# A scratch tensor in DRAM re-laid in two parts, and one more channel-major quarter in every third block, in a ConvNeXt-V2 block

## The chip, the cores and the metric

One core of a Trainium2 chip runs the whole program. The metric is device time in microseconds (us). Engines: PE (matmuls), DVE (vector), ACT (ScalarE), POOL (GpSimd), and SP (SyncE), which computes nothing and here issues most DMAs.

## The reference

```python
# x: (1, 512, 512, 96) bf16; dw: (3, 3, 96); w1: (96, 384); w2: (384, 96)
out = depthwise_conv3x3(x, dw)                       # zero padding
h = layernorm(out, axis=-1)
h = gelu(einsum('bhwc,ce->bhwe', h, w1))
gx = sqrt((h * h).sum(axis=(1, 2)) + 1e-6)           # over all pixels, per channel of 384
nx = gx / (gx.mean(axis=-1) + 1e-6)
h = grn_gamma * (h * nx) + grn_beta + h
return x + einsum('bhwe,ec->bhwc', h, w2)
```

The sum over all pixels forces two phases. Phase 1 makes everything up to the GELU and sums the squares. Phase 2 multiplies by `w2`, once the sums are known.

## The kernel before

The image is 128 blocks of four rows (`GR = 4`); a block's 2048 pixels are four quarters of 512. Phase 1 writes the normalised activations `yn` to DRAM. It reads them back transposed, with channels on the partitions, and does the first matmul and the GELU on all four quarters. One quarter's GELU output is kept in DRAM (`g_dram`); phase 2 makes the other three again from `yn`. (The last two blocks keep two quarters in SBUF.)

The squares are summed in two ways. For a *channel-major* quarter, DVE runs batch-norm statistics over its pixels. For a *pixel-major* quarter, PE multiplies the output by its own transpose (a Gram matrix, of which the diagonal counts). Two or three quarters of a block are channel-major:

```python
    def cm_quads(q):
        return 3 if q % 3 and not is_res(q) else 2
    def yn_src(q):
        return yn_dram[q].rearrange("c (r w) -> c r w", r=GR)
    def yn_rows(q):                       # what phase 2 reads: 128 x 4 runs of 768 bytes
        k = kept_quads(q) * 128
        return yn_dram[q:q + 2].rearrange("q c (r w) -> (q c) r w", r=GR)[0:128, :, k:]
    def yn_dst(q, r):
        return yn_dram[q].rearrange("(c i) (r w) -> r c i w", i=NI, r=GR)[r]
    # ...
        def stage_write(b):               # yn has partition 32 * r + c, then i, then w
            yn = yns.pop(b)
            for r in range(GR):
                sp.dma_start(out=yn_dst(b, r), in_=yn[32 * r:32 * r + 32, :, :])
        def stage_read(b):
            t = yn_ring[b % NYT]
            sp.dma_start(out=t[:C], in_=yn_src(b))
```

The work is software-pipelined in slots. SyncE's DMAs in the order of the program (shortened):

```python
            if s + 4 < NBLK:
                load_x(s + 4)                       # one DMA
            for b in get("read"):  stage_read(b)    # one DMA: the block written a slot ago
            for b in get("write"): stage_write(b)   # four DMAs
            for k in get("bcast"): stage_bcast(k)   # every fourth slot: four DMAs, 1/std to all partitions
            for k in get("rows"):  stage_rows(k)    # every fourth slot: two DMAs
            if store: store()                       # one DMA: the kept GELU output
```

## Time and profile before

The median is 1568.49 us. These lines of the profile page give busy time and share of the span for each engine, then, in 40 slices of the span, the clock granted to PE and the busy share of the 16 DMA engines, in tenths.

```profile
span 1563.2 us, 55720 instructions
PE 1450.2 (93%) x23749; PEld 844.8 (54%) x23749; DVE 1129.5 (72%) x2027; ACT 1447.1 (93%) x1306; POOL 1314.2 (84%) x933
...
PEclk9999999999999999999999999999999999999999
DMA  5668787787778677777778667869999999999993
```

The stretch from 300 to 900 us lies in phase 1, that from 1250 to 1450 us in phase 2. Columns: stretch, length, busy time of each engine (instructions), granted clock, DMA share, GB/s.

```profile
300.00:900.00 600.00, 563.83 (x10229) 283.10 (x10213) 517.70 (x878) 562.14 (x560) 532.24 (x397) 1.00 0.77 234
```

```profile
1250.00:1450.00 200.00, 197.63 (x2786) 143.72 (x2785) 104.68 (x196) 197.06 (x146) 188.35 (x116) 1.00 1.03 388
```

PE and ACT are both 94% busy in phase 1. The legend of the page warns that a busy PE isn't a PE at its peak, so look at ACT. Its timeline (start, duration, what it made, count, idle time before) shows one block per `y_bf`:

```profile
407.33 1.45 ACT L32 ACTIVATE y_bf<-Y 128x1536 bf16<-128x1536 f32 x1
408.67 2.93 ACT L32 ACTIVATE gm<-U 128x1024 bf16<-128x1024 f32 x3
412.15 2.92 ACT L32 ACTIVATE gsh<-U 128x1024 bf16<-128x1024 f32 x3 [0.55 <-PE U L32]
414.97 1.45 ACT L32 ACTIVATE y_bf<-Y 128x1536 bf16<-128x1536 f32 x1
...
422.44 1.45 ACT L32 ACTIVATE y_bf<-Y 128x1536 bf16<-128x1536 f32 x1
...
429.88 1.45 ACT L32 ACTIVATE y_bf<-Y 128x1536 bf16<-128x1536 f32 x1
```

The blocks take 7.64, 7.47 and 7.44 us: ACT does seven operations nearly back to back. One slot in three is slower, by 0.17 us. SyncE's own timeline (SPq) of two blocks:

```profile
425.91 0.41 SPq L32 DMA_DIRECT2D g_dram<-gsh  x1
426.36 0.44 SPq L32 DMA_DIRECT2D xin<-in_x_dram  x1
426.98 0.33 SPq L32 DMA_DIRECT2D ynT<-yn_dram  x1
427.35 2.55 SPq L32 DMA_DIRECT2D yn_dram<-yn  x4
429.94 2.29 SPq L32 DMA_DIRECT2D rbc<-r_dram  x4
432.33 0.86 SPq L32 DMA_DIRECT2D g_dram<-gsh  x1
433.29 0.38 SPq L32 DMA_DIRECT2D xin<-in_x_dram  x1
433.77 0.43 SPq L32 DMA_DIRECT2D ynT<-yn_dram  x1
434.25 2.49 SPq L32 DMA_DIRECT2D yn_dram<-yn  x4
```

Each write of yn takes SyncE about 0.6 us to issue. SyncE isn't counted in the busy table at all; only this timeline shows how full it is. These are its waits from 300 to 900 us (total us, times, longest):

```profile
SPq L32 <- DMA yn_dram<-yn: 73.5, 63, 4.7
SPq L32 <- POOL yn L32: 42.2, 22, 4.0
SPq L32 <- DVE rt L32: 19.7, 14, 1.9
```

Its instructions cover 381 of these 600 us, and its waits come to 205: it has slack.

### The profile page before, as it was taken

What the parts mean: (1) busy time and instruction counts of PE and PEld (TensorE: products, weight loads), DVE (VectorE), ACT (ScalarE), POOL (GpSimd) and SP (SyncE); (2) the same over time, 40 slices, a digit from 0 to 9 for tenths busy, and PEclk for the clock granted to TensorE, in tenths of its full rate; (3) what the DMA queues carried; (4) which work ended last, traced back from release to release, by engine and by line L of the source; (5) the groups of instructions that cost most, each with busy time, mean ns of one, the idle gap of its engine ahead of it and who ended that gap; (6) DMA issues with size and microseconds to landing.
All of it is one profiled execution on the core that took longest, in us unless ns stands there. A gap on an engine that the chain in (4) does not pass through costs nothing. (4 is left out here: it accounts for less than half of the span.)

```text
span 1563.2 us, 55720 instructions
## 1 busy us (share of the span) xinstructions
PE 1450.2 (93%) x23749; PEld 844.8 (54%) x23749; DVE 1129.5 (72%) x2027; ACT 1447.1 (93%) x1306; POOL 1314.2 (84%) x933
## 2 busy tenths in 40 slices
PE   7888999999999999999999997789999999999997
PEld 3444444444444444444444444457777777777765
DVE  6748978888898888889888888855555555555544
ACT  3889989999999999999999999989999999999997
POOL 3559888998989898998889897459999999999994
PEclk9999999999999999999999999999999999999999
DMA  5668787787778677777778667869999999999993
GB/s 148 182 182 269 224 262 217 240 254 227 225 234 259 210 249 244 230 235 237 247 210 243 213 197 230 268 238 387 393 379 396 387 397 388 383 381 388 379 372 147
DMA packets 235470, 427.94 MB, mean 274 GB/s; under 512 B 34102, under 2 KB 148374, under 8 KB 235222
## 3 DMA queue, kind: packets, MB, share of 16 engines
q1 hardware_dynamic: 219972, 356.59, 70.2%
q0 software_dynamic: 13888, 67.64, 11.4%
q8 instruction: 186, 3.05, 0.8%
q14 instruction: 62, 0.51, 0.1%
q10 hardware_dynamic: 1362, 0.15, 0.1%
HBM read 272.78 MB, written 150.72 MB: 271 GB/s over the span
## 5 line engine op out<-in xcount | busy, mean ns | idle before, releaser
L32 PE MATMUL U<-ynT,w1p 128*128 128x512 bf16 x2166 | 603.1, 380 | 43.5 <-ACT gm L32 8.7
L32 DVE BATCH_NORM_STATS2 bst<-gsh 128x6 f32<-128x512 bf16 x756 | 468.7, 673 | 128.9 <-ACT gsh L32 128.4
L32 ACT ACTIVATE gr<-U 128x1536 bf16<-128x1536 f32 (+1 forms) x384 | 521.0, 1450 | 17.3 <-PE U L32 14.6
L32 POOL TENSOR_TENSOR yn<-y_bf,rbc 128x1536 bf16<-128x1536 bf16 x128 | 396.9, 3103 | 81.0 <-ACT rbc L32 29.7
L32 DVE TENSOR_TENSOR o_sb<-O,xb 128x384 bf16<-128x384 f32 x512 | 277.5, 557 | 252.2 <-PE O L32 179.7
L278 POOL TENSOR_TENSOR xb<-xr,B2c 128x1536 f32<-128x1536 bf16 x126 | 394.9, 3134 | 43.4 <-DVE B2c L32 35.2
L32 ACT ACTIVATE gsh<-U 128x1024 bf16<-128x1024 f32 x378 | 369.4, 1024 | 55.8 <-ACT gm L32 29.6
L32 ACT ACTIVATE gm<-U 128x1024 bf16<-128x1024 f32 x384 | 368.1, 1035 | 0.6 <-PE U L32 0.5
L32 PE MATMUL Y<-xT,Wq 64*32 64x511 bf16 (+1 forms) x8694 | 320.9, 388 | 9.8 <-DVE B2bc_f L32 3.7
L32 POOL TENSOR_TENSOR ysq<-y_bf 128x1536 bf16<-128x1536 bf16 x114 | 313.2, 2748 | 14.0 <-ACT y_bf L32 13.4
L32 PEld LDWEIGHTS <-w1p 128*128 128x128 bf16 x2166 | 169.4, 97 | 277.9 <-issue 174.2
L32 PEld LDWEIGHTS <-gr 128*128 128x128 bf16 x4584 | 228.7, 98 | 84.4 <-ACT gr L32 12.1
L32 PE MATMUL O<-W2s,gr 128*128 128x96 bf16 x4584 | 251.3, 206 | 12.1 <-ACT gr L32 9.4
L32 PEld LDWEIGHTS <-Wq 64*32 64x32 bf16 x9216 | 102.2, 90 | 187.5 <-issue 146.9
L32 PE MATMUL U<-w1p,ynT 128*128 128x384 bf16 (+2 forms) x1032 | 161.3, 272 | 33.7 <-ACT gm L32 30.6
L32 ACT ACTIVATE y_bf<-Y 128x1536 bf16<-128x1536 f32 x121 | 175.1, 1447 | 16.6 <-PE Y L32 16.4
L32 DVE STREAM_TRANSPOSE xT<-xin 128x576 f32<-128x576 f32 (+1 forms) x256 | 181.2, 747 | 3.2 <-DMA xin<-in_x_dram 3.1
L32 DVE BATCH_NORM_STATS2 bst<-gm 128x6 f32<-128x512 bf16 x252 | 156.5, 676 | 0.9 <-ACT gm L32 0.9
L32 PEld LDWEIGHTS <-ynT 128*128 128x128 bf16 x1032 | 88.7, 96 | 90.8 <-issue 69.4
L32 PE MATMUL SG<-gm 128*128 128x128 bf16 x2064 | 136.3, 219 | 0.5 <-ACT gm L32 0.3
L32 PEld LDWEIGHTS <-gm 128*128 128x128 bf16 x2064 | 121.0, 98 | 11.5 <-issue 0.5
L250 POOL DMA_DIRECT2D xr<-in_x_dram x123 | 67.6, 549 | 27.6 <-POOL xb L278 27.6
(103 smaller groups left out, 700.3 us busy)
## 6 DMA issues: line engine op xcount, KB each, us to landing
ynT<-yn_dram SPq DMA_DIRECT2D x254, 384.0 KB
xin<-in_x_dram SPq DMA_DIRECT2D x126, 432.0 KB
yn_dram<-yn SPq DMA_DIRECT2D x512, 96.0 KB
xr<-in_x_dram POOLq DMA_DIRECT2D x128, 384.0 KB, 6.6
out_dram<-o_sb SPq DMA_DIRECT2D x127, 384.0 KB
g_dram<-gsh SPq DMA_DIRECT2D x126, 384.0 KB
gl<-g_dram SPq DMA_DIRECT2D x84, 384.0 KB
gl<-g_dram POOLq DMA_DIRECT2D x42, 384.0 KB, 6.4
```

Source lines behind the costliest of these rows:

```text
L32: r = f(*a, **k)
L250: pq.dma_start(out=xr[:], in_=x[0, r0:r0 + GR].rearrange("r w c -> (r w) c").rearrange("(p g) c -> p g c", g=PXP))
L278: pq.tensor_tensor(out=xb[:], in0=grp[q]["xr"][:], in1=bias[:, None, :].to_broadcast([128, PXP, C]), op=ALU.add)
```

## The change

The intent is twofold. The three quarters that phase 2 needs are stored together, so that phase 2 reads 3 KB runs instead of 768 B ones. And every block (but the last two) has three channel-major quarters, which takes 42 quarters of Gram work off PE. The diff, cut to its core:

```diff
     def cm_quads(q):
-        return 3 if q % 3 and not is_res(q) else 2
+        return 2 if is_res(q) else 3
@@
     def yn_rows(q):
-        k = kept_quads(q) * 128
-        return yn_dram[q:q + 2].rearrange("q c (r w) -> (q c) r w", r=GR)[0:128, :, k:]
+        n = GR * (NQ - kept_quads(q)) * 128
+        return yn_dram[q:q + 2].rearrange("q c w -> (q c) w")[0:128, :n]
-    def yn_dst(q, r):
-        return yn_dram[q].rearrange("(c i) (r w) -> r c i w", i=NI, r=GR)[r]
+    def yn_dst(q, r):
+        k = kept_quads(q) * 128
+        n = GR * (W - k)
+        dst = yn_dram[q].rearrange("(c i) w -> c i w", i=NI)
+        return [(slice(k, W), dst[:, :, r * (W - k):(r + 1) * (W - k)]),
+                (slice(0, k), dst[:, :, n + r * k:n + (r + 1) * k])]
@@
             for r in range(GR):
-                sp.dma_start(out=yn_dst(b, r), in_=yn[32 * r:32 * r + 32, :, :])
+                for cols, dst in yn_dst(b, r):
+                    sp.dma_start(out=dst, in_=yn[32 * r:32 * r + 32, :, cols])
 (cut: the same re-indexing where the matmuls read the tile)
```

A row's write is now two DMAs, one of 384 columns and one of 128.

More of the change, by code (lines that the diff above doesn't have):

```diff
@@ L101, with quad, pixel_cols @@
     MB = W // PXP
-    def quad(flat_ap, t):
-        return flat_ap.rearrange("p r (t g m) -> p t g r m", t=NQ, m=MB)[:, t]
+    def quad(yt, b, t):
+        k = kept_quads(b)
+        n = GR * (NQ - k) * 128
+        part, t, m = (yt[:, n:], t, k) if t < k else (yt[:, :n], t - k, NQ - k)
+        return part.rearrange("p (r t g m) -> p t g r m", r=GR, t=m, m=MB)[:, t]
+    def pixel_cols(b, r, t):
+        k = kept_quads(b)
+        return (r * (NQ - k) + t - k) * 128
     def quad_out(flat_ap):
         return flat_ap.rearrange("p (g r m) -> p g r m", r=GR, m=MB)
-    def yn_src(q):
-        return yn_dram[q].rearrange("c (r w) -> c r w", r=GR)
     def yn_rows(q):
+        n = GR * (NQ - kept_quads(q)) * 128
+        return yn_dram[q:q + 2].rearrange("q c w -> (q c) w")[0:128, :n]
+    def yn_dst(q, r):
         k = kept_quads(q) * 128
-        return yn_dram[q:q + 2].rearrange("q c (r w) -> (q c) r w", r=GR)[0:128, :, k:]
-    def yn_dst(q, r):
-        return yn_dram[q].rearrange("(c i) (r w) -> r c i w", i=NI, r=GR)[r]
+        n = GR * (W - k)
+        dst = yn_dram[q].rearrange("(c i) w -> c i w", i=NI)
+        return [(slice(k, W), dst[:, :, r * (W - k):(r + 1) * (W - k)]),
+                (slice(0, k), dst[:, :, n + r * k:n + (r + 1) * k])]
     consts = ctx.enter_context(tc.tile_pool(name="consts", bufs=1))
@@ L146 @@
     NYT = 6
-    yn_ring = [prepool.tile([128, GR, W], bf16, name=f"ynT{i}") for i in range(NYT)]
+    yn_ring = [prepool.tile([128, GR * W], bf16, name=f"ynT{i}") for i in range(NYT)]
     ynts = {}
@@ L212 @@
         for t in yn_ring:
-            pool.dma_start(out=t[C:128, :, :], in_=zrow[C:128, None, :].to_broadcast([128 - C, GR, W]))
+            pool.dma_start(out=t[C:128, :].rearrange("p (r w) -> p r w", w=W),
+                           in_=zrow[C:128, None, :].to_broadcast([128 - C, GR, W]))
         dve.tensor_copy(out=ident_b[:], in_=ident_f[:])
@@ L247, in stage_load @@
                 ynt = yn_ring[v]
-                sq.dma_start(out=ynt[:, :, kept_quads(q) * 128:], in_=yn_rows(q))
+                src = yn_rows(q)
+                sq.dma_start(out=ynt[:, :src.shape[1]], in_=src)
             xr = late.xr.tile([128, PXP, C], bf16, name="xr")
@@ L266, in fresh @@
                     pe.matmul(quad_out(U[:, t - nk, :]), lhsT=w1p[:, j * 128:(j + 1) * 128],
-                               rhs=quad(ynt[:], t), start=True, stop=True)
+                               rhs=quad(ynt[:], q, t), start=True, stop=True)
                 n = (NQ - nk) * QW
@@ L591, in stage_write @@
             for r in range(GR):
-                sp.dma_start(out=yn_dst(b, r), in_=yn[32 * r:32 * r + 32, :, :])
+                for cols, dst in yn_dst(b, r):
+                    sp.dma_start(out=dst, in_=yn[32 * r:32 * r + 32, :, cols])
         def stage_read(b):
             t = yn_ring[b % NYT]
-            sp.dma_start(out=t[:C], in_=yn_src(b))
+            sp.dma_start(out=t[:C], in_=yn_dram[b])
             ynts[b] = t
@@ L616, in cm_mm @@
             def cm_mm(dst, j, t):
-                pe.matmul(quad_out(dst), lhsT=w1p[:, j * 128:(j + 1) * 128], rhs=quad(yt[:], t), start=True, stop=True)
+                pe.matmul(quad_out(dst), lhsT=w1p[:, j * 128:(j + 1) * 128], rhs=quad(yt[:], b, t), start=True, stop=True)
             def pair(j):
@@ L637, in rest @@
                         t, r = divmod(k, GR)
-                        col = (cm_quads(b) + t) * 128
-                        pe.matmul(Uf[:, c - c0:c - c0 + sz], lhsT=yt[:, r, col:col + 128], rhs=w1p[:, e0:e0 + sz],
+                        col = pixel_cols(b, r, cm_quads(b) + t)
+                        pe.matmul(Uf[:, c - c0:c - c0 + sz], lhsT=yt[:, col:col + 128], rhs=w1p[:, e0:e0 + sz],
                                   start=True, stop=True)
```

## The prediction

> **What bounds the kernel now.** Phase 1 (to about 1035 us) is a loop over 128 row blocks. ScalarE's timeline from 400 to 450 us shows a block every 7.45 us where three quarters are channel-major, every 7.63 us where two are. The stretch 400 to 600 us has ScalarE 187.2 of 200 us busy, PE 188, POOL 177, DVE 172. ScalarE's work is the floor there, and the change doesn't touch it. In phase 2 ScalarE is 99.9% busy (1100 to 1300 us) with 128x1536 GELUs 1.37 us apart, PE full, POOL 94%, DMA share 1.03, 4.1 us a block.
>
> **What the change removes.** In 42 blocks a pixel-major quarter turns channel-major: 504 Gram matmuls (219 ns each) go. At most the slower block falls to the faster: 42 x 0.17 = 7 us. Phase 2 reads yn in 128 packets of 3072 B (121 ns) instead of 512 of 768 B (37 ns): 0.2 us of 16 engines a block; the share falls to about 0.98. ScalarE stays the floor, so I count 0 to 5 us, after 1300 us, where it is 98% busy.
>
> **What it adds.** (a) 126 batch-norm statistics on DVE, 0.60 us apart: 76 us. A block with three channel-major quarters takes about 7.2 of 7.45 us of DVE: it fits, barely. (b) The write of yn becomes eight DMAs a block instead of four, all issued by SyncE in program order. In its timeline four take 2.5 us (0.64 apart), with the same 96 rows each. SyncE's issue work per block is about 4.6 us (write 2.5, three large DMAs 0.4 to 0.45 each, every fourth block 2.1 for the rstd broadcast and 1.2 for its rows) and becomes about 7.2. And SyncE also stands still: it reads block b-1 back only when its write has landed, 1.8 to 5.8 us after the last issue (waits), with only 0.9 us of issues between. Each DMA also waits for a semaphore last used eight DMAs earlier (instruction order). (c) Half of the write packets are 256 B; the Trainium skill, "DMA: Bandwidth & Descriptors", Specifications, says that below 512 B there is a read-modify-write; no run here shows it yet. The DMA share of phase 1 (0.77) has room.
>
> The Trainium skill, "Perfetto Trace Analysis", What "DMA-bound" means, names this case: the issuing sequencer solid with DMA slices. SyncE isn't now; I expect it to be.
>
> **Critical path.** SyncE per block after: write 5.1, read 0.4, landing wait 1 to 1.5 not overlapped, store and x load 0.9, semaphores 0.2: 7.8 in a plain block, 8.8 with the broadcast, 8.1 on average: 0.6 over today for some 105 blocks (+60), about 1.2 for the last 15, which run at 6 us without the convolution (+18). The gain in phase 1 is hidden; phase 2 gives back 3. Sum: about +70 us.
>
> **Prediction: 1635 us, range 1578 to 1700. Faster by over 2%: 0.03; within 2%: 0.25; slower: 0.72.**
>
> **What would show it.** Phase 1 ends near 1110 us; phase 2 keeps its length within 5 us. SyncE's timeline is solid, writes 0.6 us each, its wait for the yn write the largest. ScalarE and PE fall to about 87% in phase 1; PE waits for the yn read. DVE rises to 90%, no higher.
>
> **What would make it wrong.** The 256 B writes issue faster than 0.6 us or land in under 2 us: within 2%. DVE's work delaying the transposes, or slow 256 B writes: worse than said. ScalarE held by DMA in phase 2: faster there.

## The result and the profile after

The changed kernel takes 1724.35 us (1720.07 to 1725.76, four runs); before took 1568.49. The ratio is 1.0991, 95% interval 1.0969 to 1.1012: slower. (Ratios are the mean time of one kernel's fast runs over that of the other's of the same rounds, so not quite the ratio of the medians.) The direction was right. The time lies above the range of 1578 to 1700, and the loss is 156 us where 70 was forecast.

The page after:

```profile
span 1723.2 us, 55251 instructions
PE 1481.7 (86%) x23119; PEld 835.0 (48%) x23119; DVE 1206.7 (70%) x2157; ACT 1455.4 (84%) x1306; POOL 1313.2 (76%) x933
...
PEclk8999999999999899999999999989999999999999
DMA  5557667777666677767777675576999999999994
```

The same two stretches after:

```profile
300.00:900.00 600.00, 505.31 (x8511) 240.59 (x8495) 487.77 (x827) 490.88 (x485) 461.20 (x350) 0.94 0.70 204
```

```profile
1250.00:1450.00 200.00, 200.00 (x2840) 146.91 (x2839) 108.60 (x200) 199.65 (x148) 188.36 (x115) 1.00 1.02 390
```

In phase 1 every engine in the busy table does less per microsecond, and so do the DMA engines: the limit is none of them. SyncE's timeline after:

```profile
520.49 0.54 SPq L32 DMA_DIRECT2D g_dram<-gsh  x1
521.12 1.64 SPq L32 DMA_DIRECT2D xin<-in_x_dram  x1
523.56 0.32 SPq L32 DMA_DIRECT2D ynT<-yn_dram  x1
523.93 5.04 SPq L32 DMA_DIRECT2D yn_dram<-yn  x8
529.07 1.17 SPq L32 DMA_DIRECT2D r_dram<-rt  x2
530.35 0.41 SPq L32 DMA_DIRECT2D g_dram<-gsh  x1
530.80 0.43 SPq L32 DMA_DIRECT2D xin<-in_x_dram  x1
531.41 0.33 SPq L32 DMA_DIRECT2D ynT<-yn_dram  x1
531.78 5.90 SPq L32 DMA_DIRECT2D yn_dram<-yn  x8
537.73 1.98 SPq L32 DMA_DIRECT2D rbc<-r_dram  x4
```

It is all but solid: its instructions cover 512 of the 600 us from 300 to 900 (381 before), and its waits come to 72 us instead of 205. The waits for `yn` from POOL and for `rt` from DVE are gone from the list. What is left is led by the landing of its own DMAs:

```profile
SPq L32 <- DMA xin<-in_x_dram: 16.9, 19, 2.3
SPq L32 <- DMA yn_dram<-yn: 12.4, 19, 2.3
SPq L32 <- DMA ynT<-yn_dram: 8.4, 28, 0.4
```

The other engines' waits show how SyncE's lateness spreads. GpSimd waits for the 1/std broadcast (`rbc`), which SyncE issues behind eight writes; PE and DVE then wait for GpSimd:

```profile
POOL yn L32 <- DMA rbc<-r_dram: 70.8, 10, 8.2
...
DVE rt L32 <- POOL rstd L32: 63.0, 17, 5.0
PE SG L32 <- POOL ysq L32: 61.5, 30, 3.2
```

The ends of each block's last phase 1 GELU in ACT's timeline give the time by part (us):

| part | before | after | forecast of the difference |
|---|---|---|---|
| to the end of the 5th block (ramp) | 112.7 | 116.6 | none |
| next 108 blocks, each | 7.57 | 8.79 (+132 in all) | +0.6 each, +60 |
| last 15 blocks (no convolution), each | 5.95 | 7.70 (+26 in all) | +1.2 each, +18 |
| phase 2 | 543.4 | 542.0 | 0 to -5 |

### The profile page after: what moved, and what is told of

Same layout as the page of the kernel before. It is cut to its first block, busy times and chain, and to the rows that moved or that the text cites. A ratio compares the mean times of both kernels' runs of the same rounds, so it can differ in the third digit from the quotient of the medians.

```text
span 1723.2 us, 55251 instructions
## 1 busy us (share of the span) xinstructions
PE 1481.7 (86%) x23119; PEld 835.0 (48%) x23119; DVE 1206.7 (70%) x2157; ACT 1455.4 (84%) x1306; POOL 1313.2 (76%) x933
## 5 line engine op out<-in xcount | busy, mean ns | idle before, releaser
L32 PE MATMUL U<-ynT,w1p 128*128 128x512 bf16 x2292 | 657.9, 387 | 72.1 <-ACT gsh L32 29.3
L32 ACT ACTIVATE gm<-U 128x1024 bf16<-128x1024 f32 x384 | 375.8, 1032 | 109.2 <-PE U L32 107.5
L32 PEld LDWEIGHTS <-w1p 128*128 128x128 bf16 x2292 | 181.1, 98 | 337.4 <-issue 229.4
L32 PE MATMUL Y<-xT,Wq 64*32 64x511 bf16 (+1 forms) x8694 | 329.9, 398 | 10.2 <-DVE B2bc_f L32 3.7
L32 DVE BATCH_NORM_STATS2 bst<-gm 128x6 f32<-128x512 bf16 x378 | 234.6, 676 | 1.7 <-ACT gm L32 1.7
L32 PE MATMUL U<-w1p,ynT 128*128 128x384 bf16 (+2 forms) x780 | 144.2, 300 | 29.0 <-ACT gm L32 27.6
L32 PE MATMUL SG<-rowsel,ysq 128*128 128x4 bf16 x1536 | 57.7, 167 | 108.5 <-POOL ysq L32 108.4
L32 PE MATMUL SG<-gm 128*128 128x128 bf16 x1560 | 123.2, 236 | 0.6 <-DVE SG L32 0.3
L32 PEld LDWEIGHTS <-ynT 128*128 128x128 bf16 x780 | 79.9, 106 | 72.6 <-issue 51.7
L32 PEld LDWEIGHTS <-gm 128*128 128x128 bf16 x1560 | 106.8, 107 | 14.3 <-issue 5.2
```

The costliest lines, as they stand in the source:

```text
L32: r = f(*a, **k)
```

## The experiments

Theory A: the doubled number of DMAs that SyncE must issue sets the pace. Rival B: the added statistics on DVE do. Rival C: the small write packets do. Later came theory D about a loop. Times are medians; each ratio is against runs of the kernel before in the same session.

**e1_cm_only** is the kernel before with the new `cm_quads` alone (the first hunk of the diff).

> The kernel before with three channel-major quarters in every block and nothing else changed: four writes of yn a block, old layout. Theory A (the doubled number of DMAs that SyncE must issue sets the pace of phase 1): 1558 to 1572 us, since only the up to 7 us of the faster blocks can be won. Rival B (the 126 added statistics on DVE fill it and hold up the transposes and the GELU buffers): well above 1600 us, most of the way to 1724. Rival C (small 256 B write packets): as A.

Measured: 1556.89 us, ratio 0.9937 (0.9922 to 0.9951). The median lies just under the 1558 of theory A. In the profiled runs phase 1 ends 7.0 us earlier, the very number that 42 times 0.17 us gave, but in part by luck: the middle 108 blocks give 3.2 of it, the last 15 give 2.5 and the ramp 1.3. Its stretch shows DVE at 95%, ACT as before, and the clock full:

```profile
300.00:900.00 600.00, 555.00 (x9906) 262.82 (x9905) 570.38 (x969) 565.26 (x565) 536.83 (x403) 1.00 0.76 236
```

B is refuted: this half of the change is a small gain.

**e2_layout_only** is the changed kernel with the old `cm_quads`.

> The changed kernel with the old rule of two or three channel-major quarters; the layout and its eight writes a block stay. Theory A: 1715 to 1735 us, as the changed kernel. Rival B (DVE): about 1568 us. Rival C (256 B packets): as A, so this run doesn't tell A from C.

Measured: 1721.05 us, ratio 1.0983. The whole loss is in the half of the change that re-lays yn, with its eight writes.

**e3_split512** is the kernel before with nothing changed but the count of writes:

```diff
             for r in range(GR):
-                sp.dma_start(out=yn_dst(b, r), in_=yn[32 * r:32 * r + 32, :, :])
+                for h in range(2):
+                    cols = slice(256 * h, 256 * h + 256)
+                    sp.dma_start(out=yn_dst(b, r)[:, :, cols], in_=yn[32 * r:32 * r + 32, :, cols])
```

> The kernel before with each write of yn cut in two halves of 256 columns: eight DMAs a block, packets of 512 B, none smaller, old layout, old rule, no contiguous reads. Theory A: 1700 to 1735 us. Rival C (packets of 256 B are slow to write and land late): 1568 to 1590 us. Rival B: 1568.

Measured: 1726.38 us, ratio 1.1019. The old layout, no packet below 512 B, and the same loss: C is refuted as the cause of the loss. A write of 96 KB (before) takes SyncE 597 ns (median), one of 48 KB (here) 596, and the mix of 72 and 24 KB (after) 596. The cost goes by the DMA, not by the byte. (By the number of runs in DRAM it doesn't go either: see e5.)

**e4_one_write** has the new `cm_quads`, and yn laid out in DRAM as row, channel, column. SBUF partition 32r + c and the index i then map to one contiguous DRAM row of 3 KB, so one DMA writes the block:

```diff
-    yn_dram = dram.tile([NBLK, C, GR * W], bf16, name="yn_dram")
+    yn_dram = dram.tile([NBLK, GR, C, W], bf16, name="yn_dram")
+    # read: yn_dram[q].rearrange("r c w -> c r w"); phase 2 the same, [:, :, k:], 96 rows
-            for r in range(GR):
-                sp.dma_start(out=yn_dst(b, r), in_=yn[32 * r:32 * r + 32, :, :])
+            sp.dma_start(out=yn_dram[b].rearrange("r (c i) w -> (r c) (i w)", i=NI), in_=yn[:].rearrange("p i w -> p (i w)"))
```

> Three channel-major quarters in every block, and yn laid out in DRAM as row, channel, column: the write is one DMA of 128 contiguous rows of 3 KB, the read back 384 runs of 1 KB. SyncE issues three large DMAs a block instead of six before and ten after, about 2.8 us of issue work. Theory A: not slower than before, 1545 to 1568 us, ScalarE the floor of phase 1; SyncE mostly idle. Rival B (DVE): above 1600 us. If the DMA engines or the landing of the write were the limit, it would be no better than before.

Measured: 1568.31 us (1556.17 to 1576.20), ratio 1.0005: a hair above the bounds of theory A, and not what I hoped. Phase 1 ended at 1006.0 us (before 1019.8), but phase 2 took 559.7 instead of 542 to 543. The next batch has the cause (e8).

**e5_kept_merged** is the changed kernel with the kept part in an array of its own, written by one DMA a block and read by one:

```diff
+    yk_dram = dram.tile([NBLK, GR, C, 256], bf16, name="yk_dram")
-        return [(slice(k, W), dst[:, :, r * (W - k):(r + 1) * (W - k)]),
-                (slice(0, k), dst[:, :, n + r * k:n + (r + 1) * k])]
+        return [(slice(k, W), dst[:, :, r * (W - k):(r + 1) * (W - k)])]
+            sp.dma_start(out=yk_dram[b][:, :, :k].rearrange("r (c i) w -> (r c) i w", i=NI), in_=yn[:, :, :k])
+            # and a second read, yk_dram[b][:, :, :k].rearrange("r c w -> c r w"), in stage_read
```

> The changed kernel, still with 256 B packets for the kept quarter (now also read back in 256 B runs), the contiguous 3 KB reads of phase 2 and three channel-major quarters; but the kept part of the four rows goes into its own array with one DMA. A block has five writes and two reads instead of eight and one: seven DMAs of yn instead of nine (five before). Theory A (SyncE's issue time): SyncE needs 5 x 0.64 + 2 x 0.4 + 0.9 + 0.9, about 5.8 us and 0.5 to 1 of waits, under the 7.4 of ScalarE: 1552 to 1580 us. Theory C (256 B packets): stays above 1680. Contiguous reads in phase 2 worth something: at or under 1555.

Measured: 1567.60 us, ratio 1.0005. More 256 B packets than in the changed kernel, the same contiguous reads, the same DVE work, two DMAs a block fewer: the loss is gone but for about 11 us. (The fair comparison is e1, with as many channel-major quarters and 1556.89 us; whether the two DMAs that e5 still has over e1 or the small packets cost these 11 us, no run tells.) Phase 2 took 542.4 us, so the contiguous reads are worth about nothing. The run also parts the number of DMAs from the number of runs: the one write of the kept part, 384 runs of 256 B, took SyncE 598 ns (median), as long as a write of 96 runs.

**e6_split6** is as e3, with only two of the four rows cut in halves.

> The kernel before with six writes a block (two rows cut in halves of 256 columns, two whole): the dose between four (1568) and eight (1726). Theory A as a threshold: SyncE needs about 6.7 us of issue and dispatch and some waits, just at today's 7.5 us a block: 1565 to 1605 us. If each added DMA cost the same whatever the slack, it would be half way, 1645.

Measured: 1601.62 us, ratio 1.0217 (1.0195 to 1.0238). Two more DMAs cost 33 us and four cost 158 (against the 1568.49 of before). The dose isn't proportional, as expected, but the time lies at the upper end of what I wrote: SyncE begins to cost before the ledger below shows it full.

**e7_read_later** is the changed kernel with the read back a slot later, so that SyncE doesn't stand before a write it has only just issued:

```diff
-                put(s + 2, "read", b)
+                put(s + (2 if ramp or is_res(b) else 3), "read", b)
```

> The changed kernel with the read back of a block moved one slot later in SyncE's order, so that SyncE no longer stands still for the landing of the write it has just issued. If the landing wait is a good part of the loss, as the prediction's sum had it (1 to 1.5 us a block): 1590 to 1660 us. If the issue work alone fills the block (512 of 600 us in DMA instructions plus about 0.04 us between them, 91%): 1690 to 1724 us.

Measured: 1706.47 us, ratio 1.0893. The wait for the landing, in which the prediction saw its extra, is worth 18 us of 156. In the profiled runs the middle blocks fell from 8.79 to 8.56 us, 25 us in all; the ramp, now deeper, lost 10.

**e8_one_write_128** is e4, with phase 2 reading 128 rows again (the last 32 land where the weights are zero):

```diff
-        return yn_src(q)[:, :, k:]                     # 96 rows
+        d = yn_dram[q]
+        return bass.AP(d.tensor, d.offset + k, [[W, 128], [C * W, GR], [1, W - k]])
```

> The one-write version, whose phase 1 ended at 1006 us but whose phase 2 took 560 us instead of 542, with the phase 2 read over 128 rows again (32 rows of them read in vain, as before) instead of 96. If the 96-row read made the transfers slow: phase 2 back at 542, 1545 to 1553 us in all. If the row, channel, column layout in DRAM did: 1562 to 1575 us again.

Measured: 1552.02 us (1550.05 to 1553.46), ratio 0.9904 (0.9888 to 0.9920): 1% faster than the kernel before, 10% faster than the changed one. Phase 2 is back at 542.0 us. The stretch of phase 2 in e4, then in e8:

```profile
1250.00:1450.00 200.00, 191.99 (x2717) 140.27 (x2715) 103.49 (x192) 191.88 (x142) 184.83 (x113) 1.00 1.04 353
```

```profile
1250.00:1450.00 200.00, 197.61 (x2779) 143.44 (x2776) 104.44 (x196) 197.06 (x145) 188.34 (x116) 1.00 1.03 386
```

The DMA engines are full in both and moved 9% less with the 96-row read. In the trace's packet records (1100 to 1500 us) a 3072 B packet took 137 ns on average with it and 124 without, a 768 B packet 42 and 37. Why, no run tells.

**e9_x_by_scalar** is the changed kernel with the load of x issued by ACT from block 8 on (`(sp if b < 8 else act).dma_start(...)`).

> The changed kernel with the load of x (one DMA a block from block 8 on) issued by ScalarE instead of SyncE; bytes, packets, layout and all other DMAs as in the changed kernel. Theory A: SyncE is relieved of 0.45 us of issue and 0.05 of dispatch a block, so about 115 blocks each shorten by 0.4 to 0.55: 1655 to 1685 us, although ScalarE, the floor of the kernel before, gets more to do. If the loss were in the DMA engines, in packet sizes or in landing times: unchanged, 1715 to 1730.

Measured: 1800.02 us, ratio 1.1478: a miss, in the wrong direction. SyncE's waits (300 to 900 us) tell of it:

```profile
SPq L32 <- DMA xin<-in_x_dram: 83.9, 44, 4.8
SPq L32 <- DMA yn_dram<-yn: 26.9, 47, 2.7
```

The framework gives the DMAs issued by SyncE and by ACT eight completion semaphores in turn, and a DMA must wait until the one eight before it has landed. The instruction listing of the changed kernel shows this (shortened; DMAHW0 to 7 are the eight):

```
g_dram<-gsh 128x1536 [waits DMAHW7,Activation]
xin<-in_x_dram 128x1728 [waits DMAHW0,DVE]
ynT<-yn_dram 96x2048 [waits DMAHW2,DMAHW1,PE]
yn_dram<-yn 96x1x384 [waits Pool]
yn_dram<-yn 96x1x128 [waits DMAHW3]
yn_dram<-yn 96x1x384 [waits DMAHW4]
```

With the x loads in ACT's program order, SyncE waits for ACT to reach them. So e9 is no fair test of A.

**e10_one_write_oldcm** is e8 with the old `cm_quads`.

> The one-write layout with the 128-row read of phase 2, and the old rule (two or three channel-major quarters). It completes a square: before 1567, three quarters alone 1557, one write and three quarters 1552. If the two gains add: 1560 to 1564 us. If the one write alone brings nothing, since SyncE had slack: 1566 to 1569.

Measured: 1566.14 us (1560.96 to 1574.77), ratio 1.0000 (0.9975 to 1.0024). One write alone brings nothing, since SyncE had slack. With three channel-major quarters it brings about 5 us over e1. That small interaction stays unexplained.

**e11_fill** is the changed kernel with a matmul repeated in each of the three GELU pairs (`cm_mm(U[:, 0, :], j, 0)` once more).

> The changed kernel with one of the first two matmuls of each GELU group done twice (three more 128x512 matmuls a block, same result), to keep the tensor engine busier: its granted clock fell from 1.00 to 0.94 in phase 1 of the changed kernel. Theory A: the lower clock follows from the idle tensor engine and costs nothing: 1718 to 1732 us, whether or not the clock rises. If the clock were a cause of the loss: a higher clock and a time clearly under 1710.

Measured: 1728.12 us, ratio 1.1042. The granted clock rose from 0.94 to 0.97 in the same stretch, and the time stayed:

```profile
300.00:900.00 600.00, 534.28 (x8704) 252.70 (x8697) 489.21 (x830) 491.39 (x485) 460.25 (x345) 0.97 0.70 205
```

The lower clock after the change came with an idler PE, and it isn't a visible cause of the loss.

**e12_x_by_pool** is as e9, but the x loads are issued by GpSimd, whose DMAs have semaphores of their own.

> The changed kernel with the load of x issued by GpSimd, whose DMAs use semaphores of their own (in the earlier try ScalarE's x loads took their turns among SyncE's eight semaphores, and SyncE stood waiting for them 84 of 600 us). SyncE has 0.5 us a block less to issue. Theory A, issue work plus a nearly constant wait: a block of 8.2 to 8.4 us instead of 8.8, 1660 to 1690 us in all. If SyncE's issue isn't what sets the pace: unchanged, 1715 to 1730.

Measured: 1733.90 us (1725.42 to 1744.66), ratio 1.1072: above both ranges, and again no gain. SyncE's issue work fell by 0.35 us a block, and its waits rose by 0.5. The wait before the read went from 0.22 to 0.68 us a block: the x load's issue had been filling the time in which the write lands. GpSimd also got more to do, so this isn't a clean test of A either.

**e13_more_buffers** is the changed kernel with four buffers for `yn` and `gsh` instead of three.

> The changed kernel with four buffers instead of three for yn in SBUF and for the GELU output that is stored. If SyncE's remaining 1.25 us of waiting a block comes from buffers (the engines waiting for it and it for them): 1600 to 1690 us. If it comes from the landing of its own DMAs, by the eight semaphores, and from blocks with extra issues: within 10 us of 1724.

Measured: 1719.94 us, ratio 1.0979. More of these two buffers isn't what it waits for; the other buffers were left as they were.

**e14_rstd_first** is the changed kernel with "bcast" and "rows" issued before "write" in each slot.

> The changed kernel with one swap in SyncE's program order: in each slot the rstd rows and the rstd broadcast are issued before the eight writes of yn, not after. Same DMAs, same number, same packets, same engines. Theory D, formed from the trace of the changed kernel: the pace is set by a loop that closes once in four blocks (GpSimd normalises the first block of a batch, computes the next batch's rstd, DVE turns it, SyncE stores its rows, then broadcasts it, and GpSimd waits 7.8 us for that broadcast to land), and SyncE's program order puts sixteen writes, 10 us, into this loop: 34 to 35 us for four blocks. With the swap these 10 us leave the loop and SyncE's total remains, 7.45 us a block and some waits: 1585 to 1650 us. If the sum of SyncE's issue and waits sets the pace whatever the order: 1710 to 1730.

Measured: 1741.53 us, ratio 1.1132, above both ranges. Theory D falls. GpSimd still stood idle once in four blocks, for 6.3 us where it had been 6.5 to 7.8. Its wait for the broadcast was the effect of a late SyncE, and taking that wait away only moved it.

**e15_best_rstd_first** is e8 with the same swap.

> The same swap in the one-write version (1552 us), where SyncE is idle most of the time and GpSimd waits 17 of 600 us for the broadcast. Theory D: that loop is not the limit there (ScalarE is), so nothing to 5 us: 1545 to 1553.

Measured: 1551.39 us, ratio 0.9915 (0.9902 to 0.9929): as e8.

**The ledger of SyncE**, 300 to 900 us, in us per block. It is worked out from the start and duration of each of its instructions: "issue" is a DMA's usual duration, "between" the semaphore instructions and up to 60 ns before each instruction, "waits" the rest. This rest holds two things: time in which SyncE stands before an instruction, and what an issue took beyond its usual duration.

| kernel | DMAs | issue | between | waits | block |
|---|---|---|---|---|---|
| e8_one_write_128 | 5.5 | 2.23 | 0.49 | 4.72 | 7.45 |
| before | 8.5 | 4.26 | 0.68 | 2.65 | 7.59 |
| e5_kept_merged | 10.4 | 5.24 | 0.75 | 1.42 | 7.41 |
| e6_split6 | 10.5 | 5.42 | 0.76 | 1.52 | 7.69 |
| e3_split512 | 12.3 | 6.57 | 0.83 | 1.18 | 8.57 |
| after | 12.4 | 6.60 | 0.84 | 1.25 | 8.70 |
| e7_read_later | 12.5 | 6.71 | 0.80 | 1.05 | 8.57 |
| e12_x_by_pool | 11.5 | 6.25 | 0.83 | 1.77 | 8.84 |

Down to about 6 us of issue and "between", ACT's pace of 7.4 to 7.5 rules and SyncE's waits are slack. In the changed kernel issue and "between" alone are 7.44 us, as much as ACT needs, and the waits didn't shrink below 1.05 in any run. Of the 1.25 in the changed kernel about 0.5 are time before an instruction, and about 0.75 lie inside issues that took longer than usual. Before the second to eighth write of a block SyncE stands 0.35 us a block, 56 times in the stretch, until a DMA has landed whose semaphore it needs; these writes have nothing to wait for but the DMA eight places earlier. Before the read it is 0.13 (0.22 with what the read itself took beyond its usual time).

The long issues are a cost of their own. In the changed kernel 52 of SyncE's 859 issues in the stretch took over 300 ns more than the median of their kind, 45 us together or 0.65 a block. Of these 52, 51 overlap in time with a packet of 16 KB in the queue that the profile calls "instruction" (67 such packets in the stretch, about 1.2 us each); of the other 807 issues, 52 do. Nine in ten of the long issues end 0.31 to 0.40 us after that packet. The kernel before has 40 long issues, 39 of them beside such a packet, 30 us together. (In SyncE's timeline after, above, the x load of 1.64 us and one of the eight writes that take 5.90 us are such issues.) The queue's line in the changed kernel's profile (packets, MB, share of 16 engines' span):

```profile
q8 instruction: 181, 2.97, 0.7%
```

So the long issues go with what, by the queue's name, brings instructions in. That these packets hold the issue up is not tested: no run varied them.

## Why the prediction was wrong, and where it was right

- *Right, and shown:* that the doubled number of writes is the cause (e3 has the loss with nothing else changed; e6, with six writes, a fifth of it; e5 has all else and all but 11 us of it gone); a write still takes 0.6 us to issue; DVE's added work fits "barely" (e1, 95%); the gain of phase 1 is at most 7 us (e1, 7.0, in part by luck) and hidden in the changed kernel; phase 2 keeps its length (it gave back 1.4 us, not 3, and its DMA share is 1.02, not 0.98).
- *Right, but argued:* that the number of writes acts through SyncE's issue time. The timeline and the ledger say so. Yet the two runs that took a DMA a block off SyncE (e9, e12) gained nothing, and neither is a clean test; so a cost that goes with each DMA in another way, its completion semaphore above all, isn't ruled out as a part of the loss.
- The Trainium skill, "Perfetto Trace Analysis", What "DMA-bound" means, describes the case: SyncE's instructions cover 512 of 600 us, while the DMA engines' share is 0.70.
- *The step that failed* is the term "landing wait 1 to 1.5 not overlapped" in the sum for SyncE, which put a block at 8.1 us ("0.6 over today"). Averaged over blocks with and without the broadcast it allowed about 0.85 us of waiting, nearly all for the landing of yn before the read. SyncE stands there for 0.13 us a block (0.22 with the read's own long issues), and taking that wait away (e7) shortened the middle blocks by 0.23. In its place the runs show 0.35 of waiting before the later writes and 0.65 of long issues, which the sum did not have; with small remainders the ledger's waits are 1.25. Work and gaps are 7.44, against some 7.2 forecast. So the middle blocks lost 1.22 us each, not 0.6. Between the two profiled runs the loss is 160 us, and the parts forecast add up to 75. Of the 85 between them these blocks are 72, the last 15 blocks 8 (1.75 each, not 1.2) and the ramp 4.
- *The name of the wait was wrong too.* The forecast had the wait for the yn write as the largest. It is 12.4 us of 600, and moving the read out of its way (e7) gave 18 us. Waits before the later writes are larger (24 us), by the semaphore used eight DMAs before. The prediction named that semaphore; its sum has 0.2 us a block for "semaphores". That these waits and the long issues make up the rest of the loss is argued from the ledger; no run takes either away.
- *The path was wrong:* PE was to wait for the yn read. It waits for GpSimd, which waits for the broadcast. ACT and PE fell to 82% and 84% (forecast 87), DVE is at 81%, not 90.
- *(c), the read-modify-write below 512 B* (the Trainium skill, "DMA: Bandwidth & Descriptors", Specifications) showed no step: packets of 256, 512 (e3), 768 and 1024 B (before) took 18.5, 31.7, 45.6 and 54.5 ns on average (400 to 800 us), a little more a byte for the small ones, and e5, with more 256 B packets, lost 11 us at most.
- *Open:* why SyncE's waits settle at 1.05 to 1.8 us whatever is moved (e7, e12, e13, e14). In these runs 0.56 to 0.72 us of it are the long issues, which stay. Of the rest, one wait taken away showed up as another.

## What to carry to other kernels

Count the DMAs that each issuing engine must issue per loop turn and multiply by the issue time in its timeline: this limit is in no busy table, and it costs before it is full (e6: 33 us with 6.2 of 7.7 us taken by usual issues and gaps, and 0.6 more by long ones). Look for a layout in which the SBUF partitions map to one contiguous run each, so that a whole tile is one DMA (e8: one DMA in place of four or eight, and, with e15, the best time). When one half of a change wins and the other loses, run them apart: e1 alone was a gain.

## What the Trainium skill lacked or had wrong

- "DMA: Bandwidth & Descriptors", Issuing engines are not separate DMA queues, says that the time to initiate a DMA "is usually small relative to the DMA itself". That depends on what it is set beside. A write of yn took SyncE 0.60 us to issue; it landed a median of 3.7 us after that (before, 300 to 900 us), but its 96 packets of 1 KB at 54.5 ns are only 0.33 us of 16 engines, and four more such issues a block cost 158 us (e3).
- No page gives the issue time by shape. Medians here: 0.60 us for 32 partitions of three runs each, whether 96 or 48 KB, and as much for 128 partitions of three runs (e5); 0.31 to 0.53 for a flat 96- or 128-row DMA of 384 or 432 KB.
- "Perfetto Trace Analysis", What "DMA-bound" means, advises large descriptors when the sequencer is the limit. Here the number of DMAs counted, not the descriptors' size (e3: half the size, the same issue time each; e5: four times as many runs of a quarter the size in one DMA, again the same).
- No page has it that, under the framework used here, DMAs of SyncE and ACT share eight completion semaphores in turn, so that a DMA waits for the one eight before (0.35 us a block before the later writes here; 84 of 600 us of waiting for x loads in e9).
- No page has it that a DMA issue of SyncE takes longer while a 16 KB packet of the instruction queue is under way (51 of 52 long issues, 0.65 us a block in the changed kernel).
- No page has the difference between a 96-row and a 128-row read with the DMA engines full: 353 against 386 GB/s (e4, e8).
